# Attention and gated MLP on one core: blocks of 256 tokens from the third on, two slices of d_ff to a step, two head pairs to a bank

## The chip, the core and the metric

The kernel runs on one NeuronCore of a Trainium2 chip. The figure is the device time of one execution in microseconds. A profiled execution of the kernel before is the source of every duration below; line numbers (L166) are lines of the kernel that was profiled. Engines are TensorE (PE, with its weight loads PEld), VectorE (DVE), ScalarE (ACT), GpSimd (POOL) and SyncE (SP), whose queue issues nearly all DMAs.

## The reference

```python
scores = q @ k.T / sqrt(64)              # 4 batches, 8 heads, 768 tokens, head 64
keep   = (key < n_global) | (0 <= query - key < n_local)      # 8 and 96
scores = where(keep, scores - slope[head] * distance, -1e9)
a      = softmax(scores);  x = a @ v                 # heads side by side: 3072 x 512
h      = x @ w_in                                    # 512 x 2048
g      = h * clip(h + 3, 0, 6) / 6
out    = g @ w_out                                   # 2048 x 512
```

All is float32. A kept key lies at most 95 tokens back or is one of the first 8, so a tile of 128 queries needs 232 keys (96 before it, 8 global, its own 128).

## The kernel before

**Blocks.** The 3072 tokens are eight blocks of 384 tokens, three tiles of 128 each. A block needs its attention (four pairs of heads, which fill the four 128-row parts of the transposed x) and then the two layers of the MLP. The MLP is cut along d_ff into 16 slices of 128. For a slice, `first` (L160) multiplies x by w_in into one bank: 4 parts x 3 products, since each float32 factor is split into a high and a low fp32r part and the three larger products are summed; each matmul has 128 weight columns and 384 moving columns. The gate is ACT L177, DVE L178; POOL L184 rounds the high part `gh`, DVE L191 makes the rest `gl`. `second` (L194) multiplies by w_out: per tile three matmuls with 512 moving columns, accumulated over the 16 slices in a bank per tile.

**Three stages.** (1) Until about 88 us the attention of the first three blocks (12 pairs) runs in a form of its own (`turn`, L809, L856 and L858), while DVE, ACT and POOL decode the 32 chunks of weights (`decode`); six slices of block 0 go in between; before and among the first scores PE runs matmuls on a constant (`spin`, L358) that nobody reads. (2) Until about 206 us the other slices of blocks 0 and 1 alternate. (3) From there on each block's MLP carries the attention of the next block: `attention` (L616) fills a table `units`, and after every half step (12 matmuls of `first`, or 9 of `second`) the units of that place are emitted. PE, SP and POOL execute in exactly this written order (`in_order`, L606); the scheduler may reorder DVE and ACT.

**A pair of heads in stage 3** passes through these steps. `split` (L769) makes fp32r parts of q and k: ACT L783, POOL L784, DVE L787 and L790. `scores` (L795) of tiles 0, 1, 2: four matmuls L813 each, then DVE L824 (bias and minimum), ACT L828 (exponential and sum). `sum_up` (L834): DVE L838, L839. `normalize` (L841): POOL L848, two per tile. `spread` (L863): DVE L873 transposes 32 by 32 blocks, and one DMA per tile writes them to a DRAM tile `there`. `fetch` (L878): four DMAs read them back as `weights`, now transposed; they wait for all writes of the pair. `values` (L891): the matmuls L900 multiply v by `weights` into a bank (`xp` for the first pair of two, `tp` or `sp` for the second); `put_x` (L149) makes xh on ACT and xl on DVE of it. The values of pairs 1 and 2 (counted from 1) are emitted together, and so are those of pairs 3 and 4. `weights`, `there` and `blocks` have two buffers each, the tiles of loaded q, k, v two.

Of the kernel before, what the change touches and what calls it, by code (L numbers as in the profile page):

```python
# [9 lines left out]
F32 = mybir.dt.float32  # L10
# [21 lines left out]
TG = NG + P  # L32
KW = PREV + NT * TG
QW = 2 * TB
VW = 2 * NT * P
LOAD = KW + QW + VW
# [8 lines left out]
BOTH = 10  # L45
ROOMS = 2
# [5 lines left out]
def store(nc, pool, out, row, acc, last=False):  # L52
    for tt in range(NT):
        o = pool.tile([P, DM], F32, name="o")
        nc.scalar.mul(out=o, in_=acc[tt], mul=1.0 / 6.0)
        (nc.scalar if last and tt == NT - 1 else nc.sync).dma_start(out=out[row + tt * P: row + (tt + 1) * P, :], in_=o)


class Kernel:
# [85 lines left out]
    def x_tiles(self, pool=None):  # L145
        pool = pool or self.xp
        return pool.tile([P, NKT, TB], F32R, name="xh"), pool.tile([P, NKT, TB], F32R, name="xl")

    def put_x(self, x, pair, ps):  # L149
        nc = self.nc  # L150
        xh, xl = x
        nc.scalar.copy(out=xh[:, pair, :], in_=ps)
        nc.vector.tensor_tensor(out=xl[:, pair, :], in0=ps, in1=xh[:, pair, :].bitcast(F32), op=ALU.subtract)
# [6 lines left out]
    def first(self, f, x):  # L160

        hp = self.ps_h.tile([P, BANK], F32, name="hp")[:, 0:TB]
# [8 lines left out]
    def gate(self, hp, last=False):  # L171
        nc = self.nc
        g = self.gp1.tile([P, TB], F32, name="g")
# [7 lines left out]
    def high(self, g, pool):  # L181
        gh = self.gp.tile([P, TB], F32R, name="gh")
# [6 lines left out]
    def rest(self, g, gh):  # L189
        gl = self.gp.tile([P, TB], F32R, name="gl")  # L190
# [26 lines left out]
    def acc_tiles(self):  # L217
        return [self.ps_o.tile([P, BANK], F32, name="acc") for _ in range(NT)]
# [66 lines left out]
    def load(self, n, values):  # L285

        if n < len(self.blocks) * NPAIR:
            end = KW + (TB if n < BOTH else QW)
            for columns in (slice(KW + QW, LOAD),) if values else (slice(0, KW), slice(KW, end)) if n == 0 else (slice(0, end),):
                self.nc.sync.dma_start(out=self.place(n)[:, columns], in_=self.pairs[n, :, columns])  # L290
# [8 lines left out]
    def loaded(self, n):  # L299
# [3 lines left out]
        q = at[:, KW:KW + QW].rearrange("p (j t c) -> p j t c", j=2, t=NT)  # L303
        v = at[:, KW + QW:LOAD].rearrange("p (s t c) -> p s t c", s=2, t=NT)
        return at[:, 0:KW], q, v[:, 0], v[:, 1]

# [27 lines left out]
    def banded_setup(self):  # L334
# [3 lines left out]
        self.blocks = [(b, tb) for b in range(B) for tb in range(NTB)]  # L338
# [6 lines left out]
        self.least = self.const.tile([P, 2 * NT * NPAIR * len(self.blocks)], F32, name="least")  # L345
# [87 lines left out]
    def halves(self, steps, pool=False):  # L433


        for block, f, x, acc in steps:
            self.decoded_to(2 * f)
            g = self.gate(self.first(f, x), block == len(self.blocks) - 1 and f == NF - 1)
            gh = self.high(g, pool) if pool else None
            self.work(2.1, 0.47)  # L440
            yield
            if not pool:
                gh = self.high(g, pool)
# [5 lines left out]
            self.last = (block, f, acc, gh, gl)  # L449

    def end(self, steps):

        x, acc = steps[0][2:]
        late = []
        for k, (_, f, _, _) in enumerate(steps):
            g = self.gate(self.first(f, x), f == NF - 1)
            gh = self.high(g, True)
            late.append((f, acc, gh, self.rest(g, gh)))
            if k == 0:
                self.finish()  # L460
# [519 lines left out]
```

## Time and profile before

| | |
|---|---|
| time, median of 3 runs | 668.42 us (668.13 to 668.87) |
| profiled execution | 668.19 us, span of its instructions 666.4 us |
| granted TensorE clock, mean | 0.999 |
| busy: PE, DVE, ACT, POOL | 654.5, 423.4, 278.9, 219.9 us |
| matmul records | 3963 |

The span is from the first to the last instruction; 1.8 us of the execution lie outside it. A matmul's record lasts longer than its place in the queue, because matmuls are pipelined; what counts is the distance from one start to the next, which the timeline, or a run of equal matmuls divided by their number, gives. A float32 matmul that is not fp32r (L809, L856, L900) leaves two records. An entry "idle before, releaser" of an engine tells how long it stood and what ended that.

### The profile page before, as it was taken

The numbers are of one execution on the slowest core, as the hardware profiler recorded it, in microseconds if no ns is written. First come the engines' busy times: TensorE is split into PE (matmuls) and PEld (weight loads), VectorE is DVE, ScalarE is ACT, GpSimd is POOL, SyncE is SP. The second block draws the span as 40 slices with busy tenths as digits, with TensorE's granted clock in tenths as the row PEclk, the third lists the DMA queues.
The fourth block names the chain that finished last, engine by engine and source line by source line (L and its number), as shares of the span: only waits on it lengthen the run. The fifth ranks groups of instructions, "written<-read, shape, count | busy, mean of one in ns | idle before, by whom it ended". The sixth has DMA issues, their size and how long they took to land.

```text
span 666.4 us, 11474 instructions
## 1 busy us (share of the span) xinstructions
PE 654.5 (98%) x3963; PEld 586.1 (88%) x3963; DVE 423.4 (64%) x1121; ACT 278.9 (42%) x736; POOL 219.9 (33%) x389
## 2 busy tenths in 40 slices
PE   9989999999999999999999999999999999999997
PEld 8768888888999999999999999899999999989995
DVE  6899999999234876366663886457662777422222
ACT  6898756555236333154324433143331444131111
POOL 5666622221000553043340444225340444302110
PEclk9999999999999999999999999999999999999999
DMA  8685644442003446625663366624555255510001
GB/s 288 179 253 195 198 150 135 153 134 94 1 1 134 135 139 184 174 81 138 164 154 131 86 179 164 173 80 126 155 152 137 80 150 147 138 48 2 1 1 53
DMA packets 60837, 84.74 MB, mean 127 GB/s; under 512 B 8416, under 2 KB 45536, under 8 KB 60768
## 3 DMA queue, kind: packets, MB, share of 16 engines
q1 hardware_dynamic: 60480, 83.64, 43.3%
q8 instruction: 33, 0.54, 0.3%
q14 instruction: 36, 0.29, 0.1%
q10 hardware_dynamic: 288, 0.26, 0.1%
HBM read 62.92 MB, written 20.97 MB: 126 GB/s over the span
## 4 chain that ended last, share of the span: by engine, by line
PE 81%; DVE 9%; ACT 3%; DMA 3%; issue 2%; POOL 1%; SPq 0%; ACTq 0%; DVEq 0%; POOLq 0%
PE hp L166 36%; PE acc L198 33%; DMA wst<-w 3%; PE xp L900 2%; PE sp L813 2%; PE tp L900 2%; PE tp L813 2%; ACT n L828 2%; DVE wz L402 2%; DVE wz L408 1%; DVE n L824 1%; DVE wz L394 1%; PE sp L198 1%; PE tp L198 1%; PE xp L198 1%
## 5 line engine op out<-in xcount | busy, mean ns | idle before, releaser
L177 ACT ACTIVATE g<-hp,small 128x384 f32<-128x384 f32 x127 | 73.5, 579 | 251.5 <-PE hp L166 231.9
L166 PE MATMUL hp<-xh,w1h 128*128 128x384 f32 x512 | 174.1, 340 | 0.8 <-ACT w1h L412 0.7
L166 PE MATMUL hp<-xh,w1l 128*128 128x384 f32 x512 | 172.9, 338 | 0.1
L166 PE MATMUL hp<-xl,w1h 128*128 128x384 f32 x512 | 172.0, 336 | 0.0
L184 POOL TENSOR_SCALAR gh<-g 128x384 fp32r<-128x384 f32 x96 | 51.6, 538 | 292.6 <-DVE g L178 257.4
L198 PE MATMUL acc<-w2h,gl 128*128 128x512 f32 x336 | 133.0, 396 | 0.1
L198 PE MATMUL acc<-w2l,gh 128*128 128x512 f32 x336 | 132.4, 394 | 0.0
L198 PE MATMUL acc<-w2h,gh 128*128 128x512 f32 x336 | 132.0, 393 | 0.0
L178 DVE SCALAR_TENSOR_TENSOR g<-g,hp 128x384 f32<-128x384 f32 x128 | 69.7, 544 | 86.7 <-ACT g L177 86.5
L848 POOL TENSOR_SCALAR n<-n,sums 128x232 f32<-128x232 f32 (+1 forms) x186 | 101.7, 562 | 35.7 <-DVE sums L839 21.3
L191 DVE TENSOR_TENSOR gl<-g,gh 128x384 fp32r<-128x384 f32 x128 | 78.6, 614 | 50.0 <-POOL gh L184 45.3
L828 ACT ACTIVATE n<-n,least 128x232 f32<-128x232 f32 (+1 forms) x192 | 89.1, 466 | 45.1 <-DVE least L824 43.9
L166 PEld LDWEIGHTS hp<-xh,w1h 128*128 128x128 f32 x512 | 96.3, 188 | 6.6 <-issue 1.4
L166 PEld LDWEIGHTS hp<-xl,w1h 128*128 128x128 f32 x512 | 96.2, 188 | 3.9
L166 PEld LDWEIGHTS hp<-xh,w1l 128*128 128x128 f32 x512 | 96.0, 188 | 0.4 <-DVE w1l L399 0.4
L198 PEld LDWEIGHTS acc<-w2h,gl 128*128 128x128 f32 x336 | 63.0, 187 | 14.7 <-DVE gl L191 1.0
L198 PEld LDWEIGHTS acc<-w2h,gh 128*128 128x128 f32 x336 | 63.3, 188 | 10.3 <-POOL gh L184 0.3
L198 PEld LDWEIGHTS acc<-w2l,gh 128*128 128x128 f32 x336 | 63.2, 188 | 10.3
L873 DVE STREAM_TRANSPOSE blocks<-n 128x256 f32<-128x256 f32 x112 | 43.5, 424 | 31.0 <-POOL n L848 18.7
L375 POOL TENSOR_SCALAR we<-wst 128x512 int32<-128x512 uint32 x32 | 27.8, 868 | 68.6 <-DMA wst<-w 52.2
L784 POOL TENSOR_SCALAR kx<-load 64x504 fp32r<-64x504 f32 (+1 forms) x40 | 31.0, 776 | 37.5 <-PE hp L166 35.9
L824 DVE CUSTOM_DVE_ANT_0 n<-sp,d 128x232 f32<-128x232 f32 (+1 forms) x70 | 23.6, 374 | 29.5 <-PE sp L813 29.0
(110 smaller groups left out, 780.9 us busy)
## 6 DMA issues: line engine op xcount, KB each, us to landing
wst<-w SPq DMA_DIRECT2D x32, 512.0 KB, 3.5
load<-pairs SPq DMA_DIRECT2D x22, 636.0 KB, 5.2
there<-blocks SPq DMA_DIRECT2D x52, 256.0 KB, 2.6
load<-pairs SPq DMA_DIRECT2D x32, 384.0 KB, 3.9
weights<-there SPq DMA_DIRECT2D x48, 192.0 KB, 3.8
out<-o SPq DMA_DIRECT2D x23, 256.0 KB, 2.1
weights<-there SPq DMA_DIRECT2D x32, 160.0 KB, 3.2
load<-pairs SPq DMA_DIRECT2D x9, 444.0 KB, 3.6
```

Source lines behind the costliest of these rows:

```text
L166: self.nc.tensor.matmul(hp, lhsT=self.w1(w, f)[:, kt, :], rhs=a[:, kt, :], start=(n == 0), stop=(n == 3 * NKT - 1))
L177: nc.scalar.activation(out=g, in_=hp, func=AF.Relu, bias=self.three, scale=1.0)
L178: nc.vector.scalar_tensor_tensor(out=g, in0=g, scalar=6.0, in1=hp, op0=ALU.min, op1=ALU.mult)
L184: self.nc.gpsimd.tensor_scalar(out=gh, in0=g, scalar1=1.0, scalar2=0.0, op0=ALU.mult, op1=ALU.add)
L191: self.nc.vector.tensor_tensor(out=gl, in0=g, in1=gh.bitcast(F32), op=ALU.subtract)
L198: self.nc.tensor.matmul(acc[tt], lhsT=a[:, tk], rhs=self.w2(w, f), start=(f == 0 and j == 0), stop=(f == NF - 1 and j == 2))
L375: self.nc.gpsimd.tensor_scalar(out=self.e[i], in0=words[:, :, 0].bitcast(U32), scalar1=2.0 ** -29, scalar2=0.0, op0=ALU.mult, op1=ALU.add)
L784: nc.gpsimd.tensor_scalar(out=part["kx"][own, c], in0=k[own, c], scalar1=1.0, scalar2=0.0, op0=ALU.mult, op1=ALU.add)
L824: nc.vector.tensor_tensor_reduce(out=e[:, j, lo:W], in0=sp[j][:, lo:W], in1=d, op0=ALU.add, op1=ALU.min, scale=scale, scalar=3.0e38, accum ...
L828: nc.scalar.activation(out=e[:, j, lo:W], in_=e[:, j, lo:W], func=AF.Exp, bias=self.least[:, i:i + 1], scale=-1.0, accum_out=self.sums[:, ...
L848: nc.gpsimd.tensor_scalar(out=e[:, j, lo:W], in0=e[:, j, lo:W], scalar1=over, scalar2=0.0, op0=ALU.mult, op1=ALU.add)
L873: nc.vector.transpose(out=blocks[:, :, s].rearrange("p b j q -> p j b q"), in_=e[:, :, c:c + P].rearrange("p j (b q) -> p j b q", b=4))
```

## The change

Blocks 0 and 1 stay as they are. The other 2304 tokens become nine blocks of 256 (two tiles) in place of six of 384, so that there are eleven blocks; the attention of the third block, which is done in stage 1, has two tiles for each of its four pairs. In stage 3 a step takes two slices of d_ff: `first` runs twice, into the two halves of one bank, and one gate, one `gh` and one `gl` with 512 columns serve both; then `second` runs for each slice. A step has four places for units instead of two per slice. The pairs follow each other every 7 units (6 before), where a unit is now 12 matmuls with 256 columns or 6 with 512. The values of two pairs go into the two halves of one bank and are copied by one `put_x`; they stand at unit 16 (pairs 1 and 2) and 28 (pairs 3 and 4) of 32, and for the first such block two units later. The last block ends with two slices whose gates stay apart.

```diff
+LT = 2
+LB = LT * P
+FULL = 2
+BLOCKS = [(i * TB, NT) for i in range(FULL)] + [(a, LT) for a in range(FULL * TB, B * S, LB)]
 KW = PREV + NT * TG
-QW = 2 * TB
-VW = 2 * NT * P
-LOAD = KW + QW + VW
+LOAD = KW + 2 * TB + 2 * NT * P
...
+    def first(self, f, x, hp=None):
+        if hp is None:
+            hp = self.ps_h.tile([P, BANK], F32, name="hp")[:, 0:TB]
...
-        g = self.gp1.tile([P, TB], F32, name="g")
+        n = hp.shape[-1]
+        g = self.gp1.tile([P, BANK], F32, name="g")[:, 0:n]
...
-    def second(self, f, acc, gh, gl, tiles=range(NT)):
-        for tt in tiles:
-            tk = slice(tt * P, (tt + 1) * P)
+    def second(self, f, acc, gh, gl, tiles=None, base=0):
+        for tt in range(len(acc)) if tiles is None else tiles:
+            tk = slice(base + tt * P, base + (tt + 1) * P)
...
+    def quarters(self, steps):
+        for block, f, x, acc in steps:
+            hp = self.ps_h.tile([P, BANK], F32, name="hp")
+            self.first(f, x, hp[:, 0:LB])
+            yield
+            self.first(f + 1, x, hp[:, LB:2 * LB])
+            g = self.gate(hp)
+            gh = self.high(g, True)
+            yield
+            gl = self.rest(g, gh)
+            for _ in self.finish():
+                yield
+            self.last = (block, (f, f + 1), acc, gh, gl)
...
+    def end(self, block, f, x, acc):
+        hp = [self.ps_h.tile([P, BANK], F32, name="hp")[:, 0:LB] for _ in range(2)]
         late = []
-        for k, (_, f, _, _) in enumerate(steps):
-            g = self.gate(self.first(f, x), f == NF - 1)
+        for i in range(2):
+            g = self.gate(self.first(f + i, x, hp[i]), i == 1)
             gh = self.high(g, True)
-            late.append((f, acc, gh, self.rest(g, gh)))
-            if k == 0:
-                self.finish()
-            elif k == 1:
-                self.second(*late[0], (0, 1))
-        self.second(*late[0], (2,))
-        self.second(*late[1], (0, 1))
-        self.second(*late[2], (0, 1))
-        self.second(*late[1], (2,))
-        self.second(*late[2], (2,))
+            late.append((f + i, acc, gh, self.rest(g, gh)))
+        for _ in self.finish():
+            pass
+        for t in range(LT):
+            for part in late:
+                self.second(*part, (t,))
...
     def finish(self):
-        block, f, acc, gh, gl = self.last
-        self.decoded_to(2 * f + 1)
-        self.second(f, acc, gh, gl)
-        if f == NF - 1 and block < len(self.blocks) - 1:
-            b, tb = self.blocks[block]
-            self.store(b * S + tb * TB, acc)
-        self.work(2.1, 0)
-        self.last = None
+        block, fs, acc, gh, gl = self.last
+        self.decoded_to(2 * fs[-1] + 1)
+        for i, f in enumerate(fs):
+            self.second(f, acc, gh, gl, base=i * LB)
+            if f == NF - 1 and block < len(BLOCKS) - 1:
+                self.store(BLOCKS[block][0], acc)
+            self.work(2.1, 0)
+            if f == fs[-1]:
+                self.last = None
+            yield
...
-        for i in range(2, len(self.blocks)):
+        for i in range(FULL, len(BLOCKS)):
             units, x_next = [], None
-            if i + 1 < len(self.blocks):
+            if i + 1 < len(BLOCKS):
                 x_next = self.x_tiles()
-                units, ahead = self.attention(i + 1, x_next, ahead)
-                if i == 2:
-                    units = [[]] + units
+                units, ahead = self.attention(i + 1, x_next, ahead, 2 if i == FULL else 0)
             else:
                 units = [[]] * 4 + [[lambda: self.doubt(flag)]]
-            acc = self.acc_tiles()
-            steps = [(i, f, x, acc) for f in range(NF)]
-            for k, _ in enumerate(self.halves(steps if x_next else steps[:-3], True)):
+            acc = self.acc_tiles(LT)
+            steps = [(i, f, x, acc) for f in range(0, NF, 2)]
+            for k, _ in enumerate(self.quarters(steps if x_next else steps[:-1])):
                 for unit in units[k] if k < len(units) else ():
                     unit()
             if not x_next:
-                self.end(steps[-3:])
+                self.end(*steps[-1])
...
-    def attention(self, i, x, first):
-        units = [[] for _ in range(2 * NF - 2)]
+    def attention(self, i, x, first, begin):
+        units = [[] for _ in range(2 * NF)]
         pairs = [first or Pair(self, i * NPAIR, x, False)]
         pairs[0].x = x
         if first is None:
@@ -624,20 +649,19 @@
             units[1].append(lambda: self.load_next(pairs[0].n, False))
         for p in range(NPAIR):
             n = i * NPAIR + p
-            me, after = pairs[p], Pair(self, n + 1, x, False) if n + 1 < len(self.blocks) * NPAIR else None
+            me, after = pairs[p], Pair(self, n + 1, x, False) if n + 1 < len(BLOCKS) * NPAIR else None
             pairs.append(after)
-            at = units[6 * p:]
-            for t in range(NT):
+            at = units[begin + 7 * p:]
+            for t in range(LT):
                 at[t].append(lambda t=t, me=me: me.scores(t)())
             if after:
-                at[3].append(lambda after=after: after.split(0))
-            at[3] += [me.sum_up, lambda me=me: me.normalize(0), lambda me=me: me.normalize(1)]
-            at[4] += [lambda me=me: me.normalize(2), lambda me=me: me.spread(0)]
-            at[5] += [lambda me=me: me.spread(1), lambda me=me: me.spread(2), me.fetch]
-            for t in range(1, NT if after else 0):
-                at[t + 3].append(lambda t=t, after=after: after.split(t))
+                at[2].append(lambda after=after: after.split(0))
+            at[2] += [me.sum_up] + [lambda t=t, me=me: me.normalize(t) for t in range(LT)]
+            at[3] += [lambda t=t, me=me: me.spread(t) for t in range(LT)] + [me.fetch]
+            for k in range(1, 3 if after else 0):
+                at[k + 3].append(lambda k=k, after=after: after.split(k))
             if p % 2 == 1:
-                at[11] += [lambda me=pairs[p - 1]: me.values("x"), lambda me=me: me.values("s")]
+                at[9 if p == 1 else 7].append(lambda a=pairs[p - 1], b=me: a.values("x", b))
...
-    def values(self, bank="x"):
+    def values(self, bank="x", other=None):
         nc, kk = self.nc, self.k
-        _, _, va, vb = kk.loaded(self.n)
-        xps = kk.bank(bank)[:, 0:TB]
-        for t in range(NT):
-            two = not self.low(t)
-            for c in range(2 if two else 1):
-                for j in range(2):
-                    vt, K = (va, P) if c == 0 else (vb, CB)
-                    nc.tensor.matmul(xps[j * D:(j + 1) * D, t * P:(t + 1) * P], lhsT=vt[0:K, t, j * D:(j + 1) * D],
-                                     rhs=self.part(t, j, c, K), start=(c == 0), stop=(c == 1 or not two))
-        kk.put_x(self.x, self.pr, xps)
-        kk.load_next(self.n, True)
+        width = self.nt * P
+        xps = kk.bank(bank)
+        for i, me in enumerate((self, other) if other else (self,)):
+            _, _, va, vb = kk.loaded(me.n)
+            for t in range(me.nt):
+                two = not me.low(t)
+                tk = slice(i * width + t * P, i * width + (t + 1) * P)
+                for c in range(2 if two else 1):
+                    for j in range(2):
+                        vt, K = (va, P) if c == 0 else (vb, CB)
+                        nc.tensor.matmul(xps[j * D:(j + 1) * D, tk], lhsT=vt[0:K, t, j * D:(j + 1) * D],
+                                         rhs=me.part(t, j, c, K), start=(c == 0), stop=(c == 1 or not two))
+        if other:
+            kk.put_x(self.x, slice(self.pr, self.pr + 2), xps.rearrange("p (i c) -> p i c", i=2))
+        else:
+            kk.put_x(self.x, self.pr, xps[:, 0:width])
+        for me in (self, other) if other else (self,):
+            kk.load_next(me.n, True)
```

**PE, where the values of pairs 3 and 4 stand in a block of stage 3.** In the rows, L198 (L211 after the change) is the second layer, L166 (L178) the first, L900 (L928) the values. Before:

```order
L198 MATMUL acc<-w2h_142,gh 128x512
L198 MATMUL acc<-w2l_143,gh 128x512
L198 MATMUL acc<-w2h_142,gl 128x512
L900 MATMUL xp<-weights,load_72 64x128 x12
L900 MATMUL tp<-weights,load_73 64x128 x12
L166 MATMUL hp<-xh,w1h_1391 128x384
L166 MATMUL hp<-xl,w1h_1391 128x384
L166 MATMUL hp<-xh,w1l_1392 128x384
```

After:

```order
L178 MATMUL hp<-xh_2321,w1h_1299 128x256
L178 MATMUL hp<-xl_2322,w1h_1299 128x256
L178 MATMUL hp<-xh_2321,w1l_1300 128x256
L928 MATMUL xp<-weights,load_72 64x128 x8
L928 MATMUL xp<-weights,load_73 64x128 x8
L178 MATMUL hp<-xh_2321,w1h_1299 128x256
L178 MATMUL hp<-xl_2322,w1h_1299 128x256
L178 MATMUL hp<-xh_2321,w1l_1300 128x256
```

The values now stand between the first-layer products of the last two slices. From the last scores of pair 4 to these values PE's list has in a block 48 first-layer and 45 second-layer matmuls before, 36 and 18 after; from those of pair 2 to its values it has 48, 45 and 12 matmuls of scores before, and 48, 24 and 8 after.

**POOL, around the normalisation of two pairs in turn.** L184 (L197) is `gh`, L784 (L809) the high part of the next pair's keys, L848 (L873) the normalisation. Before:

```order
L184 TENSOR_SCALAR gh<-g 128x384 x2
L784 TENSOR_SCALAR kx<-load_72 64x504 x2
L848 TENSOR_SCALAR n<-n,sums 128x232 x4
L184 TENSOR_SCALAR gh<-g 128x384
L848 TENSOR_SCALAR n<-n,sums 128x232 x2
```

After:

```order
L197 TENSOR_SCALAR gh<-g 128x512 x2
L809 TENSOR_SCALAR kx<-load_72 64x368 x2
L873 TENSOR_SCALAR n<-n,sums_6862 128x232 x4
L197 TENSOR_SCALAR gh<-g 128x512
L809 TENSOR_SCALAR kx<-load_73 64x368 x2
L873 TENSOR_SCALAR n<-n,sums_6999 128x232 x4
```

A pair's four normalisations are no longer parted by a `gh`; the `gh` of the step that runs at the time stands ahead of the keys and the normalisation, and there is one per two slices.

**SP, one pair's round trip through DRAM and the load after it.** L875 (L900) writes `there`, L882 (L907) reads it back, L290 (L304) loads q, k or v. Before:

```order
L875 DMA there<-blocks 512x1x64
L875 DMA there<-blocks 512x1x128 x2
L882 DMA weights<-there 32x4x320 x4
L290 DMA load_73<-pairs 128x1272
```

After:

```order
L900 DMA there<-blocks 512x1x64
L900 DMA there<-blocks 512x1x128
L907 DMA weights<-there 32x4x192 x4
L304 DMA load_73<-pairs 128x880
```

One write goes, the four reads stay and are smaller; there are 32 such round trips instead of 20.

More of the change, by code (lines that the diff above doesn't have):

```diff
@@ L45, with columns @@
 BOTH = 10
+LEASTS = [2 * sum(BLOCKS[i // NPAIR][1] for i in range(n)) for n in range(len(BLOCKS) * NPAIR + 1)]
+def columns(n):
+    nt = BLOCKS[n // NPAIR][1]
+    kw = PREV + nt * TG
+    return nt, kw, kw + 2 * nt * P, kw + 4 * nt * P
 ROOMS = 2
@@ L285, in load @@
     def load(self, n, values):
[L287 to L290, printed above, removed]
+        if n < len(BLOCKS) * NPAIR:
+            nt, kw, v, end = columns(n)
+            q = kw + nt * P if n < BOTH else v
+            for part in (slice(v, end),) if values else (slice(0, kw), slice(kw, q)) if n == 0 else (slice(0, q),):
+                self.nc.sync.dma_start(out=self.place(n)[:, part], in_=self.pairs[n, :, part])
     def load_next(self, n, values):
```

127 lines of the change are left out of this document (62 added, 65 removed).

## The prediction

> **What bounds the kernel now.** I read the page first, for who is busy and what the last chain runs through, then the busy times by stage, then who waited for whom.
>
> ```profile
> span 666.4 us, 11474 instructions
> PE 654.5 (98%) x3963; PEld 586.1 (88%) x3963; DVE 423.4 (64%) x1121; ACT 278.9 (42%) x736; POOL 219.9 (33%) x389
> PE 81%; DVE 9%; ACT 3%; DMA 3%; issue 2%; POOL 1%; SPq 0%; ACTq 0%; DVEq 0%; POOLq 0%
> ```
>
> The busy times by stage (length, PE, PEld, DVE, ACT, POOL, granted clock, DMA):
>
> ```profile
> 16.00:50.00 34.00, 30.30 (x321) 24.18 (x320) 30.24 (x122) 30.72 (x108) 22.10 (x46) 1.00 0.74 218
> 50.00:88.00 38.00, 35.77 (x268) 31.04 (x267) 35.53 (x90) 29.22 (x75) 21.79 (x30) 1.00 0.63 195
> 88.00:200.00 112.00, 111.64 (x555) 100.00 (x556) 87.61 (x163) 55.05 (x98) 19.97 (x22) 1.00 0.27 91
> 200.00:600.00 400.00, 400.00 (x2422) 363.20 (x2421) 243.29 (x656) 144.53 (x403) 138.04 (x240) 1.00 0.49 135
> ```
>
> From 88 us on PE is never idle, so there every start-to-start distance is on the path, and other engines' work costs nothing until PE waits for it. The distances come from the timeline of PE: one end of a block, one half step after the other.
>
> ```profile
> 565.72 0.61 PE L813 MATMUL sp<-kx,q 128*128 128x232 f32 x4
> 566.16 0.39 PE L198 MATMUL acc<-w2h,gh 128*128 128x512 f32 x1
> ...
> 568.24 0.33 PE L166 MATMUL hp<-xh,w1h 128*128 128x384 f32 x1
> ...
> 570.35 0.39 PE L198 MATMUL acc<-w2h,gh 128*128 128x512 f32 x1
> ```
>
> Four scores take 0.44 us (0.110 each, 232 columns), nine second-layer matmuls 2.08 (0.2311 each, 512 columns), twelve first-layer ones 2.11 (0.1758 each, 384 columns). What else PE could have waited for in this stage is the round trip of the normalised scores through DRAM. Who waited for whom has for the values (in us, times, longest) only this:
>
> ```profile
> PEld xp L900 <- DVE xl L153: 4.7, 6, 1.3
> PEld xp L900 <- issue: 3.8, 12, 0.4
> ```
>
> Neither names a DMA (the first is stage 1's). Now the cover of that, on a fourth pair. Its last scores, the engines' rows that carry it on, and its values:
>
> ```profile
> 410.16 0.61 PE L813 MATMUL sp<-kx,q 128*128 128x232 f32 x4
> 410.61 0.39 PE L198 MATMUL acc<-w2h,gh 128*128 128x512 f32 x1
> ```
>
> ```profile
> 412.81 1.61 POOL L784 TENSOR_SCALAR kx<-load 64x400 fp32r<-64x400 f32 x2
> 415.47 2.04 POOL L848 TENSOR_SCALAR n<-n,sums 128x232 f32<-128x232 f32 x4 [1.05 <-DVE sums L839]
> ```
>
> ```profile
> 411.45 0.08 DVE L824 DVE_READ_ACCUMULATOR2_ANT least<- 128x1 f32 x1
> 411.45 0.55 DVE L178 SCALAR_TENSOR_TENSOR g<-g,hp 128x384 f32<-128x384 f32 x1
> ...
> 415.08 0.19 DVE L839 RECIPROCAL sums<-sums 128x6 f32<-128x6 f32 x1
> ...
> 417.81 0.75 DVE L873 STREAM_TRANSPOSE blocks<-n 128x256 f32<-128x256 f32 x2
> ```
>
> ```profile
> 417.47 4.00 SPq L875 DMA_DIRECT2D there<-blocks  x3
> 423.58 1.73 SPq L882 DMA_DIRECT2D weights<-there  x4
> ```
>
> ```profile
> 429.53 1.54 PE L900 MATMUL xp<-weights,load 128*64 128x128 f32 x24
> 430.91 1.49 PE L900 MATMUL tp<-weights,load 128*64 128x128 f32 x24
> ```
>
> Count from T = 410.61, when PE goes on after the last scores. Minima end at T+0.92, the reciprocal at T+4.66, four normalisations at T+6.90, the second tile's transposes at T+7.95; the third tile's write is out by T+10.86, the reads start at T+12.97, the last 1.3 later. PE comes to pair 3's values at T+18.92 and to pair 4's at T+20.30. The trip is no shorter than about 17 us; PE fills 20 with matmuls.
>
> **The change part by part.**
>
> *First layer.* Six blocks had 6 x 192 = 1152 matmuls of 384 columns: 1152 x 0.1758 = 202.5 us. Now nine have 1728 of 256. No row has 256 columns with this operand kind; the nearest, 232, took 0.110. The line from 512 to 384 columns ends at 0.1758 - 0.0553 = 0.1205 for 256; the line from 384 to 232 gives 0.1204. I take 0.1205: 208.2 us, **+5.7**. Bounds: as cheap as the 232-column row, 190.1 us (-12.4), and for the upper one 0.130 (+22.1), my estimate of what a curve that flattens between these rows could give.
>
> [...]
>
> *Second layer.* 18 tiles x 48 matmuls before and after: **0**.
>
> *Attention that moves.* The third block loses a tile for its four pairs in stage 1; they are done in stage 3. There, PE pays per tile 0.44 for scores and a third of 1.38 (429.53 to 430.91) for values: 4 x 0.90 = 3.6. In stage 1 PE and DVE are both about 90% busy; a tile costs DVE there two minima with readout:
>
> ```profile
> L824 DVE CUSTOM_DVE_ANT_0 n<-sp,p 128x232 f32<-128x232 f32 x22 | 8.0, 389 | 0.0
> L824 DVE DVE_READ_ACCUMULATOR2_ANT least<- 128x1 f32 x192 | 15.8, 82 | 0.0
> ```
>
> 4 x 2 x 0.47 = 3.8, rounded to 4 with the smaller copies. Net **-0.4**; bounds 0 and 8 for the gain in stage 1 (where 36 tiles share some 72 us).
>
> *Gates, joint put_x, fewer instructions.* DVE, ACT and POOL do the same elements in fewer instructions; they are not on the path (the 400 us row), so **0**. A step's gate runs on 512 columns, but its `second` comes after the next step's two `first` and the previous step's two `second`, 24 x 0.1205 + 12 x 0.2311 = 5.7 us; if that cover were gone each of 64 steps would wait for what is missing. The tail after the last matmul keeps its length.
>
> *The values come sooner.* This is the term that decides. Pair 4: 36 x 0.1205 + 18 x 0.2311 = 8.50 us of matmuls after its last scores, plus pair 3's values (two tiles of three: 0.92): PE is there at T+9.42, half of the 20.30 before. The trip loses its third tile alone. With the old pace the second tile's write, now the last, goes out at T+8.0. The landings:
>
> ```profile
> there<-blocks SPq DMA_DIRECT2D x52, 256.0 KB, 2.6
> weights<-there SPq DMA_DIRECT2D x48, 192.0 KB, 3.8
> weights<-there SPq DMA_DIRECT2D x32, 160.0 KB, 3.2
> ```
>
> and for the four reads of this fourth pair alone
>
> ```profile
> DMA to landing us min/median/max: 3.0/4.0/5.1
> ```
>
> Write landed T+10.6; the reads of four follow within 1.73 us, so the last starts 1.3 later, at T+11.9; with 128 KB it takes an estimated 3.0 (the line through 192 and 160 KB gives 2.6, these reads' shortest is 3.0): T+14.9. PE **waits 5.4**. Behind the waiting values in PE's list stand the last slice's `first`, two `second` and the next block, so nothing fills the hole; DVE's xl and the gate behind it wait too, but are needed only 4 us later.
>
> Pair 2: 48 x 0.1205 + 24 x 0.2311 + 8 x 0.110 = 12.21, plus 0.92: PE is there at T+13.1. Its trip is a little longer, since POOL has the running step's `gh` ahead of the keys and the normalisation, and that `gh` cannot exist before 1.45 us of first layer, an ACT and a DVE instruction: 0.6 more, T+15.5. PE **waits 2.4**.
>
> Eight blocks have this: 8 x 7.8 = 62.4. The last of them has no next pair to split; before, that brings normalisation forward from T+4.86 to
>
> ```profile
> 568.67 1.87 POOL L848 TENSOR_SCALAR n<-n,sums 128x232 f32<-128x232 f32 x4 [0.45 <-DVE sums L839]
> 570.51 1.39 SPq L875 DMA_DIRECT2D there<-blocks  x2
> ```
>
> T+2.5 (T = 566.16): -2.4. In the first of them the values are the last thing before the next block, whose `first` then waits for put_x, an ACT and a DVE instruction: +1.5. Sum **+61.5**. Bounds: if all eight kept the pace of that last pair (second write begun at about T+5.2, reads at 2.6), pair 4 would wait 2.3 and pair 2 not at all, +18; if each set of reads took the 5.1 seen here, each wait grows by 2.1, +95.
>
> The sum is made on the profiled execution, 668.19 us (span 666.4 and 1.8 around it; 0.03% below the median of the runs): 668.2 + 5.7 - 0.4 + 61.5 = **735.0 us**, 10% slower. A difference below 0.2% could not be told from none in these runs (668.13 to 668.87).
>
> **The rivals.**
>
> *The array also goes cold in the waits.* At the start the same constant matmul, first after idling, then in the middle of work:
>
> ```profile
> 0.92 4.21 PE L358 MATMUL xp<-small 128*128 128x128 f32 x18 [0.92 <-DVE small L103]
> ...
> 14.55 0.83 PE L358 MATMUL xp<-small 128*128 128x128 f32 x6
> 15.22 0.27 PE L856 MATMUL hp<-ident,n 128*128 128x128 f32 x1
> ```
>
> 18 fill the 4.14 us up to the first scores at 5.06, 0.23 each, six fill 0.67 (the next row starts at 15.22), 0.11. So the first 4 us ran at half pace, although the profile grants 1.00. If every pair-4 wait brings this back, each costs half of 4 us: 8 x 2 = 16, **751**. For it: the wait of 5.4 is longer than the longest one before, 1.3. Against: no wait of this length inside a run is in the trace. [...]
>
> *The trip is faster than its old pace.* Two writes and smaller reads load the DMA engines less, and DVE and POOL hold less per pair: with the lower bound above, 668.2 + 5.3 + 18 = **692**. For: the last pair's rows show that pace. Against: the splits that it lacks are there in the other 31 trips.
>
> *No wait, cheaper matmuls: not slower.* If 256 columns cost what 232 do, the first layer gains 12.4 us; with the waits hidden the time is 668.2 - 12.4 - 0.4 = **655**. This wins only where pair 4 and pair 2 together wait under 1.6 us a block. Against it stands the floor of 2.3 for pair 4 from rows alone; PE's order is written out, so nothing can be pulled into the hole. With matmuls by the straight line and no wait it would be 673, still slower.
>
> **How the numbers follow.** Forecast as summed 0.52, cold array 0.25, faster trip 0.14, no wait 0.05 (faster 0.04, within 0.2% 0.01), waits beyond the bounds 0.04. The range 698 to 765 leaves out the last two and the ends of the faster trip and the cold array, about 0.2 together. Slower by over 0.2%: 0.95.
>
> **What would show it.** Right: PE's waits name DMA before the values, 16 of them, long (about 5) before pair 4's and short (2 to 3) before pair 2's; 12 first-layer matmuls of 256 columns in 1.45 us; four reads at T+10.6. Wrong: no wait for `weights`; a write of the second tile before T+5; first-layer distances of 0.11 or 0.13; waits of PE for gl, or for xl at a block's start; slow matmuls for some microseconds after a wait mean the cold array.

## The result: 758.65 us against 668.64

The changed kernel takes 758.65 us (median of four runs, 753.47 to 759.05); the kernel before, run beside it, takes 668.64 (668.13 to 669.28). The ratio is 1.1328, with a 95% interval of 1.1278 to 1.1378. That is 90.0 us more; the terms of the forecast added up to 66.8 of them.

From the page of the changed kernel: span and instructions, TensorE's row, its granted clock in 40 slices, and the shares of the chain that ended last:

```profile
span 756.8 us, 12692 instructions
PE 687.7 (91%) x4523; PEld 613.3 (81%) x4523; DVE 432.7 (57%) x1151; ACT 278.4 (37%) x729; POOL 210.3 (28%) x390
PEclk9999999999999899989989989998998998999999
PE 44%; DMA 17%; DVE 15%; issue 9%; POOL 8%; ACT 3%; SPq 3%; POOLq 0%; ACTq 0%; DVEq 0%
```

Before, PE was busy for 98% of the span and made 81% of the chain. Now it makes 44%, and the chain runs through everything that the weights pass on their way: DVE, POOL, SP's queue, DMA. By stage, with the columns that were shown of before (length, PE, PEld, DVE, ACT, POOL, granted clock, DMA):

```profile
50.00:88.00 38.00, 32.30 (x213) 26.54 (x212) 33.85 (x82) 25.00 (x62) 16.21 (x21) 1.00 0.53 168
88.00:200.00 112.00, 111.06 (x545) 99.36 (x544) 82.89 (x154) 52.11 (x92) 15.58 (x19) 0.99 0.29 90
200.00:600.00 400.00, 359.21 (x2415) 324.32 (x2415) 209.98 (x574) 124.43 (x345) 110.92 (x205) 0.94 0.41 118
```

The loss lies in stage 3. In the 400 us that PE filled before, it now idles for 40.8, and the granted clock there is 0.94 where it was 1.00. The waits of PE have a row that was not there:

```profile
PE xp L928 <- DMA weights<-there: 52.5, 15, 5.0
...
PE sp L211 <- DVE gl L204: 0.8, 1, 0.8
...
PE acc L211 <- DVE gl L204: 0.6, 1, 0.6
```

Fifteen waits for the weights' reads, 52.5 us in all, the longest 5.0, all in stage 3. The gate's `gl` was waited for twice, both times before stage 3 begins. One fourth pair in the timeline of PE, from its last scores to the matmuls after its values:

```profile
432.27 0.60 PE L838 MATMUL tp<-kx,q 128*128 128x232 f32 x4
...
441.23 1.10 PE L928 MATMUL xp<-weights,load 128*64 128x128 f32 x16
447.08 1.98 PE L928 MATMUL xp<-weights,load 128*64 128x128 f32 x16 [4.75 <-DMA weights<-there]
448.99 0.58 PE L178 MATMUL hp<-xh,w1h 128*128 128x256 f32 x1
449.37 0.41 PE L178 MATMUL hp<-xl,w1h 128*128 128x256 f32 x1
449.58 0.41 PE L178 MATMUL hp<-xh,w1l 128*128 128x256 f32 x1
...
455.05 0.28 PE L178 MATMUL hp<-xh,w1h 128*128 128x256 f32 x1
455.16 0.28 PE L178 MATMUL hp<-xl,w1h 128*128 128x256 f32 x1
```

The third pair's 16 values start at 441.23, the fourth pair's at 447.08 after 4.75 us of idling. Then comes what the forecast had left to a rival: these 16 start 0.12 us apart where the first 16 start 0.055 apart (15 distances in 0.83 us, 16 in 1.91), and first-layer matmuls start every 0.21 us; at 455 they are back at 0.12.

Summed over stage 3 from start-to-start distances, 56 us went into the gaps before the second pair's values (20 us before second pairs, 37 before fourth ones, less the matmul's own time) and some 28 into matmuls slower than those of the same shape elsewhere. The experiments separate these two and what is left.

### The profile page after: what moved, and what is told of

It reads as the page before. It is cut to its first block, busy times and chain, and to the rows that moved or that the text cites. A ratio compares the mean times of both kernels' runs of the same rounds, so it can differ in the third digit from the quotient of the medians.

```text
span 756.8 us, 12692 instructions
## 1 busy us (share of the span) xinstructions
PE 687.7 (91%) x4523; PEld 613.3 (81%) x4523; DVE 432.7 (57%) x1151; ACT 278.4 (37%) x729; POOL 210.3 (28%) x390
## 4 chain that ended last, share of the span: by engine, by line
PE 44%; DMA 17%; DVE 15%; issue 9%; POOL 8%; ACT 3%; SPq 3%; POOLq 0%; ACTq 0%; DVEq 0%
PE hp L178 20%; PE acc L211 16%; DMA weights<-there 7%; DMA there<-blocks 6%; POOL n L873 5%; PE xp L928 3%; DMA wst<-w 3%; SPq L907 3%; DVE blocks L898 2%; POOL kx L809 2%; DVE gl L204 2%; DVE wz L416 2%; DVE n L849 1%; DVE g L191 1%; DVE wz L422 1%
## 5 line engine op out<-in xcount | busy, mean ns | idle before, releaser
L178 PE MATMUL hp<-xh,w1h 128*128 128x256 f32 (+1 forms) x704 | 215.7, 306 | 2.0 <-ACT w1h L426 2.0
L178 PE MATMUL hp<-xh,w1l 128*128 128x256 f32 (+1 forms) x704 | 212.8, 302 | 0.6 <-DVE w1l L413 0.5
L178 PE MATMUL hp<-xl,w1h 128*128 128x256 f32 (+1 forms) x704 | 212.5, 302 | 0.0
L178 PEld LDWEIGHTS hp<-xh,w1h 128*128 128x128 f32 x704 | 140.1, 199 | 10.4 <-issue 4.5
L190 ACT ACTIVATE g<-hp,small 128x512 f32<-128x512 f32 (+1 forms) x104 | 67.9, 652 | 214.7 <-PE hp L178 212.3
L178 PEld LDWEIGHTS hp<-xl,w1h 128*128 128x128 f32 x704 | 140.8, 200 | 3.2
L178 PEld LDWEIGHTS hp<-xh,w1l 128*128 128x128 f32 x704 | 140.7, 200 | 1.4 <-DVE w1l L413 1.4
L197 POOL TENSOR_SCALAR gh<-g 128x512 fp32r<-128x512 f32 (+1 forms) x73 | 45.1, 618 | 346.6 <-DVE g L191 341.3
L211 PE MATMUL acc<-w2h,gh 128*128 128x512 f32 x336 | 135.6, 404 | 0.0
L211 PE MATMUL acc<-w2l,gh 128*128 128x512 f32 x336 | 133.9, 399 | 0.0
L211 PE MATMUL acc<-w2h,gl 128*128 128x512 f32 x336 | 133.1, 396 | 0.6 <-DVE gl L204 0.6
L191 DVE SCALAR_TENSOR_TENSOR g<-g,hp 128x512 f32<-128x512 f32 (+2 forms) x105 | 66.5, 633 | 73.7 <-ACT g L190 73.4
L873 POOL TENSOR_SCALAR n<-n,sums 128x232 f32<-128x232 f32 (+1 forms) x186 | 91.8, 510 | 56.0 <-DVE sums L864 52.5
L204 DVE TENSOR_TENSOR gl<-g,gh 128x512 fp32r<-128x512 f32 (+2 forms) x105 | 73.0, 695 | 36.9 <-POOL gh L197 31.3
L928 PE MATMUL xp<-weights,load 128*64 128x128 f32 (+1 forms) x480 | 39.5, 312 | 52.6 <-DMA weights<-there 52.5
L928 PEld LDWEIGHTS xp<-weights,load 128*64 128x64 f32 (+1 forms) x480 | 30.8, 155 | 58.6 <-issue 43.7
L211 PEld LDWEIGHTS acc<-w2h,gl 128*128 128x128 f32 x336 | 64.5, 192 | 16.1 <-DVE gl L204 1.5
L211 PEld LDWEIGHTS acc<-w2h,gh 128*128 128x128 f32 x336 | 66.0, 196 | 10.5
L211 PEld LDWEIGHTS acc<-w2l,gh 128*128 128x128 f32 x336 | 65.5, 195 | 9.9
L164 DVE TENSOR_TENSOR xl<-xp,xh 128x512 fp32r<-128x512 f32 (+2 forms) x28 | 17.1, 610 | 81.3 <-ACT xh L163 81.3
```

The lines of the kernel that those rows point to most:

```text
L164: nc.vector.tensor_tensor(out=xl, in0=ps, in1=xh.bitcast(F32), op=ALU.subtract)
L178: self.nc.tensor.matmul(hp, lhsT=self.w1(w, f)[:, kt, :], rhs=a[:, kt, :], start=(n == 0), stop=(n == 3 * NKT - 1))
L190: nc.scalar.activation(out=g, in_=hp, func=AF.Relu, bias=self.three, scale=1.0)
L191: nc.vector.scalar_tensor_tensor(out=g, in0=g, scalar=6.0, in1=hp, op0=ALU.min, op1=ALU.mult)
L197: self.nc.gpsimd.tensor_scalar(out=gh, in0=g, scalar1=1.0, scalar2=0.0, op0=ALU.mult, op1=ALU.add)
L204: self.nc.vector.tensor_tensor(out=gl, in0=g, in1=gh.bitcast(F32), op=ALU.subtract)
```

## The experiments

**Everything kept, TensorE busy through the wait.** The first of two sizes of the fill was too large.

```diff
         for i, me in enumerate((self, other) if other else (self,)):
             _, _, va, vb = kk.loaded(me.n)
+            if i == 1 and self.n >= 14:
+                for _ in range((34 if self.n < 42 else 20) if self.pr else 14):
+                    nc.tensor.matmul(xps[:, width:width + P], lhsT=kk.three.broadcast_to([P, P]),
+                                     rhs=kk.three.broadcast_to([P, P]), start=True, stop=True)
```

> Edit: between the first pair's weighted values and the second pair's, TensorE now runs constant matmuls (128x128, 0.11 us each) into the half of the bank that the second pair overwrites: 34 before each fourth pair (20 in the last block), 14 before each second pair but the first. They end before the weights land, so the waits for the round trip keep their places and ends; only the idle time in them is gone. Theory 1 (the array runs at half pace after an idle window, which the trace of the changed kernel puts at 28.5 us: slow values 8.3, slow first layer 16.8, slow second layer 3.4): these 28.5 go, 730 us (728 to 735), granted clock 1.00. Theory 2 (the matmuls after a wait are slow for another reason, such as operands that arrive late or DMA writes that collide with TensorE's reads): nothing changes, 756 to 762 us.

Measured: 764.06 us, ratio to before 1.1443 (1.1423 to 1.1462); clock 0.996. Neither number came. The fill's group of rows says why:

```profile
L924 PE MATMUL xp<-small 128*128 128x128 f32 x712 | 83.5, 276 | 0.0
```

Its 356 matmuls are 712 records, 82 us start to start where 56 had to be filled: one costs 0.23 us, not 0.11. No wait for `weights` is left and the pace after the values is full, so half pace did go, but the overrun took the gain back. The edit again with half as many:

```diff
-                for _ in range((34 if self.n < 42 else 20) if self.pr else 14):
+                for _ in range((17 if self.n < 42 else 10) if self.pr else 7):
```

> Edit: as keep_busy, with half as many constant matmuls (17 before a fourth pair, 10 in the last block, 7 before a second pair): one of them took 0.23 us there (two records of 0.115), not 0.11, so that 34 filled 7.8 us where the wait was 5. Now they fill 3.9, 2.3 and 1.6 us, less than each wait was (4.3 to 5.3, 2.8 and 2.0 to 3.75). Theory 1 (half pace follows idle time): the slow matmuls go, which measured against spacing_6 are 24 us (first layer 15.4, second layer 3.6, the rest in the values), the waits stay: 735 us (731 to 739). Theory 2 (the matmuls after a wait are slow for another reason): 756 to 762 us.

Measured: **735.57 us** (733.47 to 738.44), 1.1015 (1.098 to 1.105). Its waits, and the matmuls after the same fourth pair's values:

```profile
PE xp L931 <- DMA weights<-there: 9.4, 12, 2.0
```

```profile
436.26 1.10 PE L931 MATMUL xp<-weights,load 128*64 128x128 f32 x16 [0.74 <-DMA weights<-there]
437.30 0.39 PE L178 MATMUL hp<-xh,w1h 128*128 128x256 f32 x1
437.52 0.28 PE L178 MATMUL hp<-xl,w1h 128*128 128x256 f32 x1
437.64 0.28 PE L178 MATMUL hp<-xh,w1l 128*128 128x256 f32 x1
```

The values still end when the weights have landed, but behind them the first layer runs at 0.12 us at once. So 23.1 us of the rise were half pace (758.65 - 735.57), and idling caused it: with the same transfers, and values that wait for them as before, filling the idle time alone removes it. The medians are from two rounds, beside which the kernel before took 668.64 and 667.68 us, so the figure is good to a few us; in the two profiled runs stage 3 is 23.0 us shorter. One window of half pace is left in stage 3, behind the longest wait of 2.0 us (granted clock 0.57 between 499.59 and 503.00 us).

**Values later in the block.**

```diff
-                at[9 if p == 1 else 7].append(lambda a=pairs[p - 1], b=me: a.values("x", b))
+                at[(9 if begin else 11) if p == 1 else (7 if begin else 10)].append(lambda a=pairs[p - 1], b=me: a.values("x", b))
...
-        self.attending(self.ctx, 2, 3, 2, side="right")
+        self.attending(self.ctx, 2, 3, 3, side="right")
```

> Edit: from the fifth block's attention on, the values of the first two pairs come 2 units later (one first-layer and one second-layer piece, 2.8 us) and those of the last two pairs 3 units later (one first-layer and two second-layer pieces, 4.2 us), the very end of a block; a third buffer holds the weights that are then alive. Theory 1 (TensorE waits for a round trip that takes as long as before): of waits of 2 to 3.7 us before a second pair and 4.3 to 5.3 before a fourth some 0 to 0.9 and 0 to 1.1 are left, no idle stretch is long enough for half pace, and about 1 us per block comes in for the x of the last two pairs at the next block's start: 689 us (680 to 698). Theory 2 (the trip itself is held up by something that moves with the values, such as a buffer that they free): the waits stay, above 735.

Measured: 692.73 us, 1.0384 (1.0362 to 1.0405), inside the range of theory 1.

```profile
PE xp L928 <- DMA weights<-there: 6.3, 4, 4.6
...
PE hp L178 <- DVE xl L164: 2.4, 7, 0.3
```

Four waits for the weights are left, of which 4.6 us belong to the first block, whose values were not moved at the fourth pair. The second row is new: the values stand at the very end, so the next block's `first` waits for their `xl`, as the forecast had feared for the first block. The twelve matmuls of that `first` take 2.17 us instead of 1.43.

**No wait for the trip.**

```diff
+        self.fixed = self.pool("fixed", 1, side="right").tile([P, 4, LT, 2, 2, 32], F32, name="fixed")
+        self.nc.gpsimd.memset(self.fixed, 0.01)
...
     def part(self, t, j, c, K):
...
-        return self.weights[0:K, :, t, 1 - c, j]
+        return self.k.fixed[0:K, :, t, 1 - c, j]
```

> Edit: the values of all pairs from the fourth block on read a constant buffer instead of the weights that come back from DRAM; scores, normalisation, transposes, writes and reads all still run, but nothing waits for them (the attention part of the output is left out in this way). Theory 1 (56.1 us of waits and 28.5 us of half pace after them are the whole rise but 6): 674 us (671 to 678). Theory 2 (the 256-column matmuls, the extra instructions or the gates cost a large part of it): over 690 us.

Measured: 681.29 us, 1.0201 (1.0184 to 1.0218): 7 us above the expectation, and still below the other theory's bound. Some 2 of the 7 look like the edit's own, a wait at the start of stage 3 that the kernels beside it lack, where POOL has the constant to fill ahead of the keys:

```profile
PE sp L840 <- DVE kx L817: 2.3, 2, 1.9
```

Another 1.6 stand ahead of stage 3, which starts at 204.95 us here and at 203.33 in the changed kernel: stage 1 has one more window of half pace here (from 74.45 us; the granted clock between 50 and 88 us is 0.96, and 1.00 in the changed kernel). From its first matmul to the last, stage 3 takes 12.0 us more than before, 9.7 without that wait. So 674 was too low: without any wait for the trip stage 3 costs more than the 6 us that were allowed for it.

**A pair every 6 units, values 12 units after their scores.** This keeps everything and gives the round trip 15.5 us of layers.

```diff
-            at = units[begin + 7 * p:]
+            at = units[begin + 6 * p:]
...
-                at[9 if p == 1 else 7].append(lambda a=pairs[p - 1], b=me: a.values("x", b))
+                at[12 if p == 1 or not begin else 10].append(lambda a=pairs[p - 1], b=me: a.values("x", b))
...
-        self.attending(self.ctx, 2, 3, 2, side="right")
+        self.attending(self.ctx, 2, 3, 3, side="right")
```

> Edit: a pair every 6 units instead of 7, and the values 12 units after the first scores of their second pair (9 and 7 before; 10 for the last two pairs of the first such block), with a third buffer of weights. TensorE then has 15.5 us of layers plus a pair's values between the last scores and the values that read their weights, against a trip that landed 13.2 to 14.4 us (fourth pair) and 15.4 to 16.6 us (second pair) after the last scores. Theory 1 (only the time between scores and values is short): no waits, no half pace, 674 us (671 to 682). Theory 2 (the trip gets slower when the pairs stand closer, since DVE, POOL and the queue of reads have less time for each): waits of 2 us and more come back, over 690 us.

Measured: **678.67 us** (678.37 to 679.99), 1.0169 (1.0152 to 1.0186).

```profile
span 677.1 us, 12702 instructions
PE 659.8 (97%) x4523; PEld 589.5 (87%) x4523; DVE 432.5 (64%) x1151; ACT 277.1 (41%) x729; POOL 212.1 (31%) x390
PE 81%; DVE 9%; DMA 4%; ACT 2%; issue 2%; POOL 1%; POOLq 0%; SPq 0%; ACTq 0%; DVEq 0%
```

PE is back at 97% and 81% of the chain, and no wait of PE names a DMA. The trips landed 12.3 to 17.2 us after the last scores, most of them at 12.8 to 14.9 (12.0 to 17.1 in the changed kernel): closer pairs did not slow them. 80.0 us of the rise are thus the place of the values and the spacing of the pairs, 56.9 as waits (735.57 - 678.67, which still has one window of half pace) and 23.1 as half pace. The kernel before took 667.76 us beside this run, so 10.9 us remain; the parts add up to 90.9 and not 90.0 because it took 0.9 us more beside the changed kernel.

**The same fault put into the kernel before.**

```diff
-                at[11] += [lambda me=pairs[p - 1]: me.values("x"), lambda me=me: me.values("s")]
+                at[8] += [lambda me=pairs[p - 1]: me.values("x"), lambda me=me: me.values("s")]
```

> Edit, made to the kernel before (blocks of 384 tokens, one slice a step, a bank for each pair): the values of two pairs come 3 units earlier, 8 after the first scores of the second of them and not 11, which takes 6.3 us from the 18.8 to 20.1 us between last scores and values. Its trips landed 16.9 to 20.2 us after the last scores (second pair) and 16.4 to 19.3 (fourth pair). Theory 1 (what costs is values ahead of the round trip, whatever the size of a block): ten waits of about 4.5 and 5.5 us, 50 us, and half pace after them, 10 x 1.5 to 2: 735 us (722 to 748). Waits without half pace: 717 us. Theory 2 (the rise comes from 256-token blocks or the joint bank): 668 to 672 us.

Measured: 733.41 us, 1.0980 (1.0961 to 1.0998). The ten waits stand in two rows, one for each of the banks that scores use:

```profile
PE tp L900 <- DMA weights<-there: 22.8, 5, 6.3
PE sp L900 <- DMA weights<-there: 20.2, 5, 5.2
```

43.0 us of waits in a rise of 65.7, where 50 had been expected. Most of the rest is again half pace, more than the 15 to 20 expected: 16 windows of 3.41 us ran at half clock, with 43.6 us of work in them, which loses 21.8 us. Blocks of 384 tokens with a bank for each pair suffer the same way, so neither the block's size nor the joint bank is the cause, except in that a step of 256 tokens gives a trip less time.

**The joint bank undone** (in the kernel with a pair every 6 units).

```diff
-            if p % 2 == 1:
-                at[12 if p == 1 or not begin else 10].append(lambda a=pairs[p - 1], b=me: a.values("x", b))
+            at[12 if p < 3 or not begin else 10].append(lambda me=me: me.values("x"))
```

> Edit, made to spacing_6: the joint bank is undone; each pair has its values and its x by itself, 12 units after its own first scores (10 for the last pair of the first such block). Theory 1 (the joint bank only saves changes between kinds of matmul, about 0.1 us into and 0.1 out of the values, 16 groups more here): 678.7 + 3 = 682 us (680 to 684). Theory 2 (it matters for more, such as x ready for the next block or fewer instructions on VectorE): over 685 us; a joint bank that costs something: under 678 us.

Measured: 683.32 us (682.53 to 685.53), 4.6 more than 678.67. The joint bank is a gain of about that size, together with the later place of the first pair's values that it brings (6 units); about 3 us were expected from changes between kinds of matmul, and no run separates the two.

**Stage 1: decoding earlier** (in the same kernel). Two edits ask where the time of the four tiles went that stage 1 no longer computes.

```diff
+                        elif n + 2 < EARLY:
+                            self.work(0 if n + 2 < BOTH else 0.78, 0)
...
+                        elif 0 <= n < EARLY:
+                            self.work(0.396, 0)
```

> Edit, made to spacing_6: where the third block has no third tile in stage 1, the planner of the weights' decoding is still given that tile's TensorE time (0.78 and 0.396 us, and nothing on VectorE), so that as many decoding steps are set there as if the tile were there and more. In the changed kernel stage 1 ended no sooner although four pairs have a tile less; between 55 and 112 us TensorE waits there 2.0 us for a decoded w1h, 2.0 for normalised scores and 0.5 for w1l, and runs 3.3 us at half pace behind that. Theory 1 (the work taken out of stage 1 comes back as a wait for decoding that is set too late): 2 to 4 us less than spacing_6 (678.7), 675 to 677 us. Theory 2 (VectorE, 89% busy in 50 to 88 us, is the bound there, so earlier decoding only moves the wait to the scores): 678 to 681 us.

```diff
-LEAD = 6
+LEAD = 3
```

> Edit, made to spacing_6: decoding of the weights gets a head start of 3 us in the planner's account (LEAD 3 in place of 6), all through stage 1. Theory 1 (decoding is late at the end of stage 1): as decode_kept, 675 to 677 us. Theory 2 (VectorE is full there): no gain, or a loss where the decoding delays the first pairs: 678 to 682 us.

Measured: 678.30 us (676.69 to 679.73) and 678.20 (678.05 to 678.36) against 678.67: no gain that could be told. The waits of PE between 55 and 112 us, first with a pair every 6 units alone, then with the head start (`LEAD = 3`):

```profile
PE hp L178 <- ACT w1h L426: 2.1, 2, 1.7
PE tp L881 <- POOL n L873: 2.0, 2, 1.5
...
```

```profile
PE sp L834 <- DVE least L849: 1.3, 1, 1.3
PE tp L881 <- POOL n L873: 1.0, 2, 0.6
PE acc L211 <- DVE gl L204: 0.2, 1, 0.2
```

The first edit left both of the first two rows as they are, 2.1 and 2.0 us, so it did not bring the decoding forward where it was wanted and decides nothing. With the head start the wait for `w1h` is gone there, but the decoding done sooner takes its time earlier. Between 16 and 50 us PE has less done with the head start (the second row) than without:

```profile
16.00:50.00 34.00, 30.00 (x317) 23.94 (x316) 30.39 (x120) 30.20 (x103) 23.34 (x46) 1.00 0.66 195
16.00:50.00 34.00, 27.62 (x266) 21.56 (x264) 30.58 (x116) 29.21 (x97) 22.67 (x43) 0.94 0.61 192
```

There PE idles for 3.3 us in one place, before values of stage 1 (no releaser is named for it), and two windows of half pace follow, from 46.0 to 52.8 us, with 6.5 us of work in them:

```profile
PE xp L928 <- issue: 3.3, 1, 3.3
```

So the head start gained nothing as it was done here; whether late decoding is what keeps stage 1 long is not settled, since what it took away came back in another place.

Where the 4 us went that the forecast had given to stage 1 can be read, if not why. Between 55 and 112 us PE waits for 5.7 us in the changed kernel and for 2.1 in the kernel before. And behind the wait for `w1h` a window of half pace stands, which the kernel before does not have; here with a pair every 6 units (PE busy, granted clock, DMA):

```profile
82.99:86.40 3.41, 1.70 (x16) 1.00 0.57 193
86.40:89.81 3.41, 2.97 (x10) 0.50 0.26 29
89.81:93.23 3.42, 3.42 (x18) 1.00 0.62 199
```

In the changed kernel it is the window from 87.68 us, with 3.41 us of work, so 1.7 us lost. What sets the waits stays open: VectorE is busy for about 90% between 50 and 88 us in both kernels, which fits theory 2, but it too lost work with the four tiles, and no run tested it by itself.

## Why the prediction was right on the sign and where it fell short

*What bounds it.* Right. The forecast's main term, the round trip through DRAM against the matmuls that cover it, is what the chain, the waits and three of the experiments show. For the pair in the timeline, T = 432.71: PE came to the fourth pair's values at T+9.35 (T+9.42 forecast), the reads were issued from T+9.8 on (T+10.6), and the weights had landed at T+14.2 (T+14.9). What the transfers took, by size:

```profile
there<-blocks SPq DMA_DIRECT2D x56, 256.0 KB, 2.6
weights<-there SPq DMA_DIRECT2D x96, 128.0 KB, 3.0
weights<-there SPq DMA_DIRECT2D x32, 96.0 KB, 2.4
```

The reads of 128 KB took the estimated 3.0 us.

*The values come sooner, +61.5.* Right in size: 56.9 by the runs, in 15 waits where 16 were named. Fourth pairs waited 4.3 to 5.3 (5.4), the last one 2.8 (3.0); second pairs 2.0 to 3.75 (2.4), but the first of them only 0.4, since its trip landed at 13.4 us where later ones took 14.7 to 16.7. The 1.5 us for `x` at the start of the block behind it is 0.7 in the run with the shorter fill, where half pace does not cover it: that block's first twelve matmuls take 2.17 us there, not 1.43.

*First layer, +5.7.* Right within its bounds. At full pace twelve matmuls of 256 columns take 1.43 us, 0.1195 each, where the straight line gave 0.1205; over 1728 that is +3.5 against 203.0 before, and +4.8 with what the first matmul after a group of values costs (with a pair every 6 units; in the timeline with the shorter fill it starts 0.22 us ahead of the next one, not 0.12).

*Attention that moves, -0.4.* Wrong, by some 6 us in two terms. The 4 us that stage 1 was to give back did not come: stage 3's first matmul starts at 203.33 us (202.72 before), with 3.6 us more of waits between 55 and 112 us and a window of half pace, and the two runs on decoding could not bring it out. And the attention of stage 3, +3.6 forecast, is +5.6 with a pair every 6 units (scores +2.5, values +3.1). With the first layer's +4.8, the later start of stage 3 in that run (+0.8), the second layer's -0.2 and a tail shorter by 0.4, that is 10.6, against 10.9 between the medians; the forecast had 5.3.

*No half pace in the sum.* This is the step that failed: the forecast put a term that came to 23.1 us at nothing. It kept half pace as the rival "the array also goes cold in the waits", at a chance of 0.25 and 16 us. It happened, and cost 23.1. The reason given against it, that no wait of this length is in the trace, was no evidence: the trace of before had no such wait to show. The sizing was short as well, since it gave half pace to fourth pairs only and 4 us to each. It followed all eight waits of fourth pairs, but four of second pairs too, of 2.65 to 3.75 us, and seven of the twelve spells outlasted one window (below).

*The other rivals.* The trip was not faster by enough: 692 needed pair 2 without a wait. "No wait" is excluded by the waits' row. "Beyond the bounds" did not happen to the waits.

So the sum of the forecast, term by term against the runs: waits 61.5 and 56.9; half pace 0 and 23.1; all else 5.3 and 10.9. That the shortfall is so nearly the half pace alone is luck: waits 4.6 us too high and other terms 5.6 us too low cancel.

## What to carry to other kernels

When a step gets shorter, everything whose cover was counted in steps gets less time: convert the distance from producer to consumer into microseconds of the new step, and compare it with the old trip, before anything else. If that comparison leaves TensorE idle at a place that comes back, for as long as the waits that half pace followed here, put half pace into the sum, not among the rivals (here twelve waits of 2.65 us and more brought it; two of 2.0 us, one of 0.4 and one of 2.8 did not). And work taken out of a stage in which two engines are 90% busy is no gain until a run shows which of them the stage waits for.

## What the runs showed of the hardware

**Half pace in windows of 3.413 us.** In the changed kernel the slow stretches start and end on one grid of 3.413 us, over the whole of stage 3: the ends of the spells near 265.2, 452.9 and 702.1 us are 55 and 73 such steps apart. Cut on that grid, from 234.46 to 708.91 us, 120 windows have a granted clock of 1.00 and 19 of 0.50, none one between (length, PE busy, granted clock, DMA). A fourth pair:

```profile
442.67:446.08 3.41, 0.00 (x0) 1.00 0.64 172
446.08:449.50 3.42, 2.42 (x18) 0.50 0.60 190
449.50:452.91 3.41, 3.41 (x15) 0.50 0.40 77
452.91:456.32 3.41, 3.41 (x21) 1.00 0.00 0
```

and two second pairs with waits of 3.3 and 2.8 us:

```profile
415.36:418.78 3.42, 2.34 (x27) 1.00 0.54 126
418.78:422.19 3.41, 1.48 (x19) 1.00 0.77 234
422.19:425.60 3.41, 3.41 (x15) 0.50 0.75 200
```

```profile
606.51:609.92 3.41, 2.15 (x26) 1.00 0.62 150
609.92:613.34 3.42, 2.14 (x25) 1.00 0.72 214
613.34:616.75 3.41, 3.41 (x20) 1.00 0.89 229
```

In these traces the idling in a window at full clock goes with the clock of the next. In stage 3, 1.93 us or more was followed by half clock (12 times here, 10 times in the kernel before with early values), 1.27 or less never. Three other traces narrow it. In the kernel before with early values 1.65 us were followed by full clock:

```profile
602.26:605.67 3.41, 1.76 (x26) 1.00 0.65 145
605.67:609.08 3.41, 0.27 (x5) 1.00 0.83 201
609.08:612.50 3.42, 3.42 (x29) 0.51 0.05 9
```

With the shorter fill 1.79 us (the window from 495.70 us) were followed by half clock, and so were 1.71 us in stage 1 with a pair every 6 units (the window from 82.99 us, shown above). So of the windows read in these traces 1.65 us is the longest idling that full clock followed, and 1.71 us the shortest that half clock followed from full.

The way back in stage 3, in the same two kernels: windows at half clock with 0.58 us of idling or more were followed by another at half, and full clock came only after a window without any. Stage 1 differs: with a pair every 6 units a window with 0.44 us of idling (86.40 us, above) was followed by full clock, with the head start one with 0.34 us (45.99 us) by half. No run shows what tells these two apart.

So in the changed kernel the wait of 2.65 us from start to start, which idles for 2.38 us inside the window from 671.36 us, was followed by one window at half clock, and the one of 2.8 us, whose 2.54 us of idling a boundary cuts into 1.26 and 1.27, by none; the seven of 4.3 to 5.3 us, which all reach into a second window, were followed by two windows each. In stage 3 of the changed kernel 19 windows ran at half clock, with 55 us of work in them, which loses some 27 us at half the pace; the fill gave back 23.1 and left one such window.
